# Banded attention and a gated dense layer on one core: the same instructions in another order

## The chip, the cores and the metric

The kernel runs on one core of a Trainium2 chip. The metric is the device time of one launch in microseconds (us). The kernel before takes 725.28 us, the median of three runs (724.6 to 726.31).

## The reference

The first half is attention over a band with a few sink columns: 4 batches, 8 heads, 768 positions, head size 64, `n_sink` 4 and `window` 128.

```
scores = np.matmul(q, k.transpose(0, 1, 3, 2)) / np.sqrt(D)
is_sink = pos[None, :] < n_sink
in_window = (rel >= 0) & (rel < window)          # rel = query position - key position
scores = np.where(is_sink | in_window, scores, -1e9)
a = softmax(scores); attn_out = a @ v             # (4, 8, 768, 64)
```

The second half takes the eight heads of a position as one row of 512 and puts it through two dense layers, with a gate between them:

```
x = attn_out.transpose(0, 2, 1, 3).reshape(3072, 512)
h = x @ w_in                                      # (3072, 2048)
g = h * np.cos(h)
out = g @ w_out                                   # (3072, 512)
```

`q`, `k` and `v` are float32. The weights arrive as 64-bit floats and are read as pairs of 32-bit words.

## The kernel before

**Tiles.** A float32 product is made of three TensorE products of parts: each operand is split into a high part and the low rest (`xhi`, `xlo`, `whi_in`, `wlo_in`, `ghi`, `glo`, `whi_out`, `wlo_out`), and high x high, high x low and low x high are summed in PSUM. The 3072 rows are cut into 12 chunks of 256 rows. The first four are the first 256 rows of each batch, whose heads are called early heads; they read keys and queries in their natural layout (L947) and turn them on TensorE (L955). The other eight chunks come later and share work between heads. Two chunks form a dense pair, d = 0 to 5, of 512 rows. A pair is worked off in 16 slots, one for each 128 columns of `h`. A slot is 12 matmuls of 128x512 into `h` (L476), a half sine on ScalarE (L485), a square (L491 on ScalarE or L493 on VectorE), the gate (L498), the split of g into `ghi` (L507, ScalarE) and `glo` (L514, VectorE), and 12 matmuls into four accumulators `acc` j = 0 to 3 (L523), which a later slot issues. In names such as `ghi_92` the number only tells allocations apart; `acc_80_1` is accumulator 1 of the last pair. The last slot keeps its g in the space of `whi_in`, so that its accumulator matmuls read `acc<-whi_out,whi_in`.

**Weights.** They come in 32 pieces of 128x512. A piece is loaded as pairs of words into one of two raw buffers (`raw0`, `raw1`, L580 on the SyncE queue), decoded on VectorE in three instructions (L595, L601, L607), rounded to its high part on ScalarE (L628), and its low part is taken by VectorE or GpSimd (L631). A load waits until its raw buffer is free, and what stands behind it on the SyncE queue waits with it.

**Checks.** The fast path holds only for inputs in some range. Late in the run the kernel reads weights again (L646) and values again (16 loads on SyncE, squares on ScalarE, L668, sums on VectorE, L671, all through the buffer `raw1` at the end) and gathers their extremes. When all are there, VectorE takes the maximum (L1665, L1669), TensorE turns it (`most_t`, L1675), VectorE reduces it (L1678), TensorE turns it again (`row_t`, L1682), and ten small VectorE instructions (L273 to L276, L1687 to L1697; the first four need nothing of the result) write the flag `redo`. Every engine then loads this flag into a register (`TENSOR_LOAD`, L1844) and branches on it (L1845): to a general path, which does not run with these inputs, or to the end of the program, which copies the last pair's four accumulators out of PSUM (L533 for j = 0 to 2 on ScalarE, for j = 3 one half by ScalarE, L543, and one by VectorE, L545) and stores them (L552).

**What sets the order.** No order is written by hand. Class `Plan` holds a list of steps, each with the engines that could do it, a planned duration, what it needs, and a priority (a planned time). `Plan.order` walks through planned time and lets each free engine take the ready step with the lowest key, which is the priority and penalties for a second choice of engine. The instructions of each engine then run on the chip in just that order. Priorities are made of the numbers in table `C`: `head_time(g)` from `TH`, `HB`, `TH2`, `HO` and `T`; `slot_time(d, s)` from `H0`, `STEP` and `T`; and offsets for the steps within a head or slot (`DQ`, `DS`, `DX`, `DH`, `DM`), the weight pieces (`WI`, `WO`, `WS`, `LEAD`) and the checks (`CK`, `CL`, `CV`, `CS`, `CT`, `CE`). Sixty idle matmuls (L1556) have the lowest priority and fill TensorE's first stretch. Three lines show the form:

```
i = add(dma(2), load_values, [r], prio - C["CL"], lat=2.6)
t, bt, bt2 = slot_time(len(ys) - 1, NFT - 1) + C["CE"], buf("tp", 1), buf("tp", 1)
i = add([("PE", 0.11)], most_turn, [i, bt], t)
```

Of the kernel before, what the change touches and what calls it, by code (L numbers as in the profile page):

```python
# [24 lines left out]
MASKED = 8.0e9  # L25

C = {
# [4 lines left out]
    "POOLF": 0.999, "POOLPEN": 2.492, "R": 2, "RAW": 2, "SAME": 0.056, "SEM": 0.352, "SPE": -0.019, "STEP": 7.601,  # L32
# [3 lines left out]
}  # L36
MAX_NORM = 39.0
MIN_TOP = 1.125 * 2.0**-15
# [1842 lines left out]
```

## Time and profile before

| | |
|---|---|
| Median of three runs | 725.28 us |
| Profiled execution | 727.14 us, span 725.3 us, granted clock 0.998 |
| Busy, share of the span | PE 707.8 us (98%), DVE 599.3 (83%), ACT 527.3 (73%), POOL 127.0 (18%) |
| Chain that ended last, by engine | PE 78%, ACT 12%, DVE 5%, issue 2%, DMA 2% |
| Traffic | HBM read 69.86 MB, written 6.29 MB |

The time of a run is the span of the profile and 1.84 us around it. The chain by engine says what the last work hung on: mostly TensorE (PE), and beside it ScalarE (ACT), VectorE (DVE) and a little DMA. A busy share is a mean over stages, so the rows below give the stages apart.

### The profile page before, as it was taken

The numbers are of one execution on the slowest core, as the hardware profiler recorded it, in microseconds if no ns is written. First come the engines' busy times: TensorE is split into PE (matmuls) and PEld (weight loads), VectorE is DVE, ScalarE is ACT, GpSimd is POOL, SyncE is SP. The second block draws the span as 40 slices with busy tenths as digits, with TensorE's granted clock in tenths as the row PEclk, the third lists the DMA queues.
The fourth block names the chain that finished last, engine by engine and source line by source line (L and its number), as shares of the span: only waits on it lengthen the run. The fifth ranks groups of instructions, "written<-read, shape, count | busy, mean of one in ns | idle before, by whom it ended". The sixth has DMA issues, their size and how long they took to land.

```text
span 725.3 us, 12983 instructions
## 1 busy us (share of the span) xinstructions
PE 707.8 (98%) x3674; PEld 583.6 (80%) x3674; DVE 599.3 (83%) x1850; ACT 527.3 (73%) x1344; POOL 127.0 (18%) x213
## 2 busy tenths in 40 slices
PE   7888999999999999999999999999999999999997
PEld 6766787888888888888888888888888888888885
DVE  6889999998988978988978989888988875567763
ACT  3796886787797697796686886877887856566652
POOL 1010000000333222232231232232122322100000
PEclk9999999999999999999999999999999999999999
DMA  5665565533255333355433254533244410375651
GB/s 144 177 181 162 140 178 148 155 67 66 63 118 130 86 67 54 64 125 128 93 58 59 42 144 101 122 63 62 44 124 107 111 35 12 96 198 158 167 138 63
DMA packets 236500, 77.11 MB, mean 106 GB/s; under 512 B 221060, under 2 KB 221060, under 8 KB 236420
## 3 DMA queue, kind: packets, MB, share of 16 engines
q1 hardware_dynamic: 236128, 75.15, 43.5%
q10 hardware_dynamic: 292, 1.05, 0.5%
q8 instruction: 31, 0.51, 0.3%
q14 instruction: 49, 0.40, 0.2%
HBM read 69.86 MB, written 6.29 MB: 105 GB/s over the span
## 4 chain that ended last, share of the span: by engine, by line
PE 78%; ACT 12%; DVE 5%; issue 2%; DMA 2%; SPq 0%; ACTq 0%; DVEq 0%
PE h L476 30%; PE acc L523 30%; PE av L1239 4%; PE s L1048 4%; ACT p L1079 3%; PE s L992 2%; PE tp L1160 2%; PE av L1215 2%; DMA xk<-in_k_dram 2%; ACT p L1097 1%; ACT L485 1%; ACT L1079 1%; PE qk L955 1%; PE tp L1170 1%; ACT early L390 1%
## 5 line engine op out<-in xcount | busy, mean ns | idle before, releaser
L523 PE MATMUL acc<-whi_out,ghi 128*128 128x512 f32 x376 | 158.7, 422 | 0.0
L476 PE MATMUL h<-xhi,whi_in 128*128 128x512 f32 x384 | 155.3, 405 | 0.0
L476 PE MATMUL h<-xlo,whi_in 128*128 128x512 f32 x384 | 150.9, 393 | 0.0
L476 PE MATMUL h<-xhi,wlo_in 128*128 128x512 f32 x384 | 150.1, 391 | 0.0
L523 PE MATMUL acc<-whi_out,glo 128*128 128x512 f32 x376 | 147.8, 393 | 0.0
L523 PE MATMUL acc<-wlo_out,ghi 128*128 128x512 f32 x376 | 147.1, 391 | 0.0
L1198 POOL TENSOR_SCALAR_AFFINE_SELECT ph<-ph 128x512 fp32r<-128x512 f32 x128 | 87.2, 681 | 230.9 <-DVE ph L1191 227.1
L485 ACT ACTIVATE r<-h 128x512 f32<-128x512 f32 x96 | 57.1, 598 | 47.9 <-PE h L476 45.3
L476 PEld LDWEIGHTS h<-xlo,whi_in 128*128 128x128 f32 x384 | 72.1, 188 | 16.2
L523 PEld LDWEIGHTS acc<-whi_out,glo 128*128 128x128 f32 x376 | 70.6, 188 | 15.8
L476 PEld LDWEIGHTS h<-xhi,whi_in 128*128 128x128 f32 x384 | 72.3, 188 | 12.0 <-DVE r L498 0.3
L476 PEld LDWEIGHTS h<-xhi,wlo_in 128*128 128x128 f32 x384 | 72.5, 189 | 11.3
L523 PEld LDWEIGHTS acc<-whi_out,ghi 128*128 128x128 f32 x376 | 71.4, 190 | 10.4
L1079 ACT ACTIVATE p<-p,st 128x136 f32<-128x136 f32 (+1 forms) x192 | 79.3, 415 | 0.3
L523 PEld LDWEIGHTS acc<-wlo_out,ghi 128*128 128x128 f32 x376 | 71.3, 190 | 9.2
L498 DVE SCALAR_TENSOR_TENSOR r<-r,h 128x512 f32<-128x512 f32 x96 | 64.5, 674 | 16.9 <-ACT r L491 16.3
L507 ACT CAST ghi<-r 128x512 fp32r<-128x512 f32 x94 | 58.2, 619 | 19.6 <-PE acc L523 12.7
L514 DVE TENSOR_TENSOR glo<-r,ghi 128x512 fp32r<-128x512 f32 x94 | 65.3, 694 | 5.6 <-ACT ghi L507 4.9
L1070 DVE CUSTOM_DVE_ANT_0 p<-s,mk 128x136 f32<-128x136 f32 (+1 forms) x192 | 59.7, 313 | 6.2 <-PE s L992 2.8
L1008 ACT CAST l<-tq 64x256 fp32r<-64x256 f32 x64 | 25.8, 403 | 46.9 <-PE s L1048 46.4
L1056 DVE COPY_PREDICATED s<-mk,s 128x128 f32<-128x128 int32 x128 | 37.2, 291 | 25.6 <-PE s L1048 23.7
L1048 PEld LDWEIGHTS s<-r,l 128*128 128x128 f32 x256 | 46.4, 188 | 12.3 <-DVE ph L1191 1.4
(161 smaller groups left out, 1314.7 us busy)
## 6 DMA issues: line engine op xcount, KB each, us to landing
xk<-in_k_dram SPq DMA_DIRECT2D x256, 48.0 KB
raw<-in_moe_w_out_dram SPq DMA_DIRECT2D x16, 512.0 KB
wt<-in_moe_w_in_dram SPq DMA_DIRECT2D x32, 256.0 KB
raw<-in_moe_w_in_dram SPq DMA_DIRECT2D x14, 512.0 KB
v<-in_v_dram SPq DMA_DIRECT2D x64, 96.0 KB
raw<-in_v_dram SPq DMA_DIRECT2D x32, 192.0 KB
out_dram<-wt SPq DMA_DIRECT2D x22, 256.0 KB
wt<-in_moe_w_out_dram SPq DMA_DIRECT2D x20, 256.0 KB
```

The costliest lines, as they stand in the source:

```text
L476: nc.tensor.matmul(out=o.h, lhsT=w[:, c, fs], rhs=xx[:, c, :], start=(c == 0 and n == 0), stop=(c == NC - 1 and n == 2),)
L485: nc.scalar.activation(out=o.r, in_=o.h, func=AF.Sin, scale=0.5)
L498: nc.vector.scalar_tensor_tensor(out=o.r, in0=o.r, scalar=0.5, in1=o.h, op0=ALU.subtract, op1=ALU.mult)
L507: nc.scalar.copy(out=o.ghi, in_=o.r)
L514: e.tensor_tensor(out=o.glo, in0=o.r, in1=f32(o.ghi), op=ALU.subtract)
L523: nc.tensor.matmul(out=y.acc[j], lhsT=gg[:, j * P : (j + 1) * P], rhs=w[:, f, :], start=(f == 0 and n == 0), stop=(f == NFT - 1 and n == 2),)
L1048: nc.tensor.matmul(out=o.s_ps[j][:, :w], lhsT=o.l[:, j * P : (j + 1) * P], rhs=r.rearrange("p n s -> p (n s)")[:, c0 : c0 + w], start=(n = ...
L1056: nc.vector.copy_predicated(out=o.s_ps[j][:, :P], mask=below.bitcast(I32), data=o.s_ps[j][:, SW : SW + P])
L1070: nc.vector.tensor_tensor_reduce(out=o.pj[j][:, :w], in0=o.s_ps[j][:, :w], in1=masks[min(o.i0 + j, 2)][:, :w], op0=ALU.add, op1=ALU.min, s ...
L1079: nc.scalar.activation(out=o.pj[j][:, :w], in_=o.pj[j][:, :w], func=AF.Exp, bias=o.lead.st[:, 0, o.nth, j : j + 1], scale=-1.0, accum_out= ...
L1198: nc.gpsimd.affine_select(out=ph[:, :, b, :], in_=f32(ph)[:, :, 1, :], pattern=[[0, 2 * CB], [(-1, 1)[b], P]], compare_op=(ALU.is_gt, ALU. ...
L1239: nc.tensor.matmul(out=dst, lhsT=lhs, rhs=rhs, start=(n == 0), stop=(n == len(seq) - 1), skip_group_check=True)
```

## The change

Only the table `C` differs. No step is added or taken away; the numbers that make the priorities are others, and the planner gives another order from them. Two lines of it:

```
-    "CT": 8.22, "CS": -0.257, "CE": -3.976, "H0": 21.541, "HB": 1.252, "TH2": 7.345, "GA": 16, "GHI": 2, "GLO": 2,
+    "CT": 14.939, "CS": -0.447, "CE": -7.191, "H0": 24.38, "HB": 0.716, "TH2": 7.156, "GA": 16, "GHI": 2, "GLO": 2,
...
```

Changed besides are `ALT`, `BLF`, `CK`, `DA`, `DH`, `DM`, `DQ`, `DS`, `DV`, `DX`, `CV`, `CL`, `HO`, `SX`, `CR`, `LEAD`, `NM`, `NW`, `NWF`, `PEN`, `POOLF`, `POOLPEN`, `SAME`, `STEP`, `T`, `TH`, `P0`, `A0`, `G0`, `S0`, `ZV`, `LD`, `HOT`, `RL`, `K2`, `WI`, `WO`, `WS`, `WS2` and `VP`. The table's `FILL`, `R`, `RAW`, `WT`, `PB`, `L` and the other buffer counts stay.

**TensorE, end of the list.** Before, the two turns of the check's result (`most_t`, `row_t`) stand between accumulator matmuls of slot 92's g, with 39 matmuls behind the second:

```order
L523 MATMUL acc_80_1_7949<-wlo_out_92,ghi_92_8472 128x512
L523 MATMUL acc_80_1_7949<-whi_out_91,glo_92_8485 128x512
L1675 MATMUL most_t_8534<-ident_77,most_93 33x128
L523 MATMUL acc_80_2_7956<-whi_out_91,ghi_92_8472 128x512
L523 MATMUL acc_80_2_7956<-wlo_out_92,ghi_92_8472 128x512
L523 MATMUL acc_80_2_7956<-whi_out_91,glo_92_8485 128x512
L1682 MATMUL row_t_8541<-ident_77,row_94 1x33
L523 MATMUL acc_80_3_7963<-whi_out_91,ghi_92_8472 128x512
```

After, the rows up to the branch are these:

```order
L523 MATMUL acc_80_3_7958<-whi_out_91,whi_in_89 128x512
L523 MATMUL acc_80_3_7958<-wlo_out_92,whi_in_89 128x512
L523 MATMUL acc_80_3_7958<-whi_out_91,whi_in_89 128x512 x2
L523 MATMUL acc_80_3_7958<-wlo_out_92,whi_in_89 128x512
L523 MATMUL acc_80_3_7958<-whi_out_91,whi_in_89 128x512
L1675 MATMUL most_t_8580<-ident_77,most_93 33x128
L1682 MATMUL row_t_8583<-ident_77,row_94 1x33
L1844 TENSOR_LOAD redo_86
L1845 COMPARE_AND_BRANCH
```

Both turns have moved behind the last accumulator matmul; nothing but the load of the flag and the branch follows them.

**VectorE, end of the list.** The last value sum (L671), the maxima and the work that leads to the flag; before, they stand ahead of the last slot's gate (`r_95`):

```order
L514 TENSOR_TENSOR whi_in_89<-r_94_8493,whi_in_89 128x512
L671 TENSOR_REDUCE yt_79<-raw1_71 128x12
L1665 TENSOR_REDUCE most_93<-yt_79 128x32
L1669 TENSOR_REDUCE most_93<-yt_79 128x1
L1678 TENSOR_REDUCE row_94<-most_t_8534 33x1
```

After, the gate and `glo` of the last slot (`whi_in`) come first, and the last value sum and the rest behind them:

```order
L671 TENSOR_REDUCE yt_79<-raw1_71 128x12
L498 SCALAR_TENSOR_TENSOR r_95_8523<-r_95_8523,h_95_8496 128x512
L514 TENSOR_TENSOR whi_in_89<-r_95_8523,whi_in_89 128x512
L671 TENSOR_REDUCE yt_79<-raw1_71 128x12
L1665 TENSOR_REDUCE most_93<-yt_79 128x32
L1669 TENSOR_REDUCE most_93<-yt_79 128x1
L1678 TENSOR_REDUCE row_94<-most_t_8580 33x1
L273 TENSOR_TENSOR lims_83<-sm_81,lims_83 1x4
```

The check's own chain is the same, but begins behind the last slot's work.

**SyncE, front of the list.** Loads of queries and keys for the early heads (`xq`, `xk`), raw weight pieces and values, from row 9 on. Before:

```order
L947 DMA xq_74<-in_q_dram 128x2x64 x2
L947 DMA xk_75<-in_k_dram 128x2x64 x2
L580 DMA raw1_71<-in_moe_w_in_dram 128x1024
L947 DMA xq_74<-in_q_dram 128x2x64 x2
L580 DMA raw0_70<-in_moe_w_out_dram 128x1024
L947 DMA xk_75<-in_k_dram 128x2x64 x2
L947 DMA xq_74<-in_q_dram 128x2x64 x2
L928 DMA vpe_153<-in_v_dram 128x2x64
L947 DMA xk_75<-in_k_dram 128x2x64 x2
L928 DMA v32_76<-in_v_dram 128x2x64
```

After:

```order
L947 DMA xq_74<-in_q_dram 128x2x64 x2
L947 DMA xk_75<-in_k_dram 128x2x64 x2
L580 DMA raw1_71<-in_moe_w_in_dram 128x1024
L947 DMA xq_74<-in_q_dram 128x2x64 x2
L947 DMA xk_75<-in_k_dram 128x2x64 x2
L580 DMA raw0_70<-in_moe_w_out_dram 128x1024
L928 DMA vpe_153<-in_v_dram 128x2x64
L947 DMA xq_74<-in_q_dram 128x2x64 x2
L947 DMA xk_75<-in_k_dram 128x2x64 x2
L928 DMA v32_76<-in_v_dram 128x2x64
```

The first load of a `w_out` piece (into `raw0`) now stands behind a pair of key loads instead of ahead of it, and the first value load (`vpe`) ahead of a pair of `xq` and a pair of `xk`.

**VectorE, front.** From the start to the copy `tk` (L392) that releases the score matmul ahead of the first dense matmul, VectorE's list had 129 instructions and now has 126: one each fewer of L595, L601 and L607, two fewer of L392 with 64x256, one fewer of L392 with 128x384, and three more of L1099 with 128x128. ScalarE's list up to the last high part of x (L349) that the first dense matmul reads had 92 instructions and now has 90. All 60 idle matmuls stand ahead of the first dense matmul in both orders, and one score matmul more does now. Slots 2 to 14 of the first pair have 2 to 4 us more of the heads' matmuls ahead of them than before; from slot 15 on the two orders are level again. Three low parts of `w_out` pieces (L631) go from VectorE to GpSimd.

## Rows read from the trace of the kernel before

**Rows 1.** Windows: stretch, its length, PE, PEld, DVE, ACT, POOL busy, clock, DMA share, GB/s

```profile
20.00:57.00 37.00, 32.30 (x187) 24.98 (x187) 31.04 (x108) 33.05 (x113) 3.43 (x4) 1.00 0.65 171
57.00:170.00 113.00, 110.79 (x554) 89.10 (x555) 105.34 (x283) 84.47 (x205) 1.22 (x4) 1.00 0.52 137
170.00:620.00 450.00, 448.75 (x2401) 373.32 (x2399) 383.87 (x1253) 346.54 (x903) 119.09 (x192) 1.00 0.39 83
620.00:720.50 100.50, 100.48 (x451) 81.86 (x449) 64.39 (x153) 56.95 (x106) 0.72 (x1) 1.00 0.52 141
```

**Rows 2.** Chain that ended last: start us, us, what

```profile
43.42 3.85 DMA xk<-in_k_dram
57.32 1.39 PE h L476 x6
...
711.37 9.12 PE acc L523 x39
...
720.51 0.39 ACT raw L543
...
721.01 0.42 DVE raw L545
```

**Rows 3.** Timeline of TensorE at the end: start us, us, instruction

```profile
710.29 0.27 PE L1675 MATMUL most_t<-ident,most 128*33 128x128 f32 x1
...
720.09 0.39 PE L523 MATMUL acc<-whi_out,whi_in 128*128 128x512 f32 x1
```

**Rows 4.** Timeline of VectorE at the end

```profile
702.04 0.95 DVE L671 TENSOR_REDUCE yt<-raw 128x12 f32<-128x768 f32 x1
...
708.11 0.95 DVE L671 TENSOR_REDUCE yt<-raw 128x12 f32<-128x768 f32 x1
...
709.37 0.21 DVE L1669 TENSOR_REDUCE most<-yt 128x1 f32<-128x64 f32 x1
...
712.29 0.15 DVE L1697 SCALAR_TENSOR_TENSOR redo<-row_t,sm 1x1 int32<-1x1 f32 x1
```

**Rows 5.** Line L533 from 700 us on: ScalarE's first instruction behind the branch

```profile
L533 ACTq EVENT_SEMAPHORE  x3: 17/17/937, 716.2 to 717.8; - x3
```

**Rows 6.** Flag's load, L1844: queue, ns min/median/max, first and last start us

```profile
L1844 POOLq TENSOR_LOAD <-redo x1: 489/489/489, 712.5 to 712.5; - x1
```

**Rows 7.** Branch, L1845, and GpSimd's first instruction behind it

```profile
L1845 POOLq COMPARE_BRANCH  x1: 45/45/45, 713.0 to 713.0; - x1
L1845 ACTq COMPARE_BRANCH  x1: 50/50/50, 713.6 to 713.6; - x1
...
L1845 POOLq EVENT_SEMAPHORE  x1: 17/17/17, 715.6 to 715.6; - x1
```

**Rows 8.** Timeline of ScalarE at the end

```profile
709.81 0.60 ACT L485 ACTIVATE r<-h 128x512 f32<-128x512 f32 x1 [1.73 <-PE h L476]
...
717.16 1.23 ACT L533 ACTIVATE wt<-acc 128x512 f32<-128x512 f32 x2 [3.48 <-PE acc L523]
```

**Rows 9.** VectorE by line and form up to 57 us: busy us, mean ns, idle before

```profile
L607 DVE SCALAR_TENSOR_TENSOR wt<-raw,wt 128x512 int32<-128x512 int32 x10 | 6.8, 683 | 0.1
...
L595 DVE TENSOR_SCALAR wt<-raw 128x512 int32<-128x512 int32 x10 | 4.2, 419 | 2.3 <-DMA raw<-in_moe_w_in_dram 2.2
L392 DVE COPY early<-qk 64x256 f32<-64x256 f32 x6 | 2.5, 425 | 3.3 <-ACT tk L390 1.7 <-PE qk L955 1.0 <-ACT early L390 0.6
...
L392 DVE COPY early<-tp 128x384 f32<-128x384 f32 x3 | 1.7, 553 | 0.0
...
L1099 DVE TENSOR_SCALAR p<-p,st 128x128 f32<-128x128 f32 x2 | 0.6, 282 | 0.0
```

**Rows 10.** Timeline of SyncE's queue in front: start us, us, DMA issue

```profile
19.86 1.71 SPq L580 DMA_DIRECT2D raw<-in_moe_w_out_dram  x1
21.67 0.90 SPq L947 DMA_DIRECT2D xk<-in_k_dram  x2
```

**Rows 11.** SyncE's waits up to 57 us: total us, times, longest us

```profile
SPq L928 <- PE av L1215: 3.3, 4, 1.2
```

More of the change, by code (lines that the diff above doesn't have):

```diff
@@ L27 @@
 C = {
[4 rows of a table removed]
-    "POOLF": 0.999, "POOLPEN": 2.492, "R": 2, "RAW": 2, "SAME": 0.056, "SEM": 0.352, "SPE": -0.019, "STEP": 7.601,
[3 rows of a table removed]
[4 rows of a table added]
+    "POOLF": 1.007, "POOLPEN": 3.979, "R": 2, "RAW": 2, "SAME": 0.061, "SEM": 0.352, "SPE": -0.019, "STEP": 7.814,
[3 rows of a table added]
 }
```

12 rows, old and new, of the table C are left out of this document.

## The prediction

> **What bounds the kernel now.** I read the windows by stage first. TensorE is the engine to watch: from 170 to 620 us it is idle for 1.25 us of 450, from 620 us to its last matmul for 0.02 of 100.5, and from 57 to 170 us for 2.2 of 113 [rows 1]. There a new order can give back nearly nothing, since the same matmuls take the same time. Idle time lies in two places: ahead of the first dense matmul at 57.3 us [rows 2], where TensorE does without 4.7 us of 37 and ScalarE (33.05 of 37) and VectorE (31.04 of 37) are as full [rows 1], and behind the last matmul. So I read the front and the end apart.
>
> At the end the chain of waits shows an unbroken run of 39 accumulator matmuls from 711.37 us on, then ScalarE's half copy at 720.51 and VectorE's, which ends at 721.43 [rows 2]. The last matmul starts at 720.09 [rows 3] and the span ends at 725.3, so 5.2 us lie behind it. The check's two turns stand far ahead of that: `most_t` at 710.29 [rows 3], the flag written at 712.29 + 0.15 = 712.44 [rows 4], and load, branch and jump were over on ScalarE at 716.2 [rows 5], while TensorE still had 4 us of matmuls in hand. All of the decision is hidden.
>
> **The change, the end.** In the new order both turns stand behind the last accumulator matmul. Neither the flag nor any branch can come before it, and the four copies and stores stand behind the branch. Counted from the start of the last accumulator matmul:
>
> - to `most_t`: one matmul spacing, 9.12/39 = 0.23 [rows 2];
> - `most_t` to the flag: 712.44 - 710.29 = 2.15 [rows 3, 4]. The four VectorE instructions that need nothing of the result still stand behind the first reduction, so this chain keeps its length;
> - flag to the end of the compare: load at 712.5 and 0.49 long [rows 6], compare 0.05 [rows 7], so 713.04 - 712.44 = 0.60;
> - the jump: ScalarE's compare ends at 713.65 [rows 7] and its first instruction behind it is at 716.2 [rows 5]: 2.55. It is no wait for data, since GpSimd, which has nothing to wait for, shows the same (713.0 + 0.05 to 715.6, [rows 7]);
> - three copies of 128x512 in a row on ScalarE at 1.23/2 [rows 8]: 1.85. Before, they were spread between the matmuls that fill the four accumulators;
> - ScalarE's half and VectorE's half: 721.43 - 720.51 = 0.92 [rows 2];
> - last store to the end of the span: 725.3 - 721.43 = 3.87.
>
> The sum is 12.17 us against 5.21 before, so 6.96 more. The two turns no longer stand between the accumulator matmuls; I take one matmul spacing, 0.23, for both, so that much comes off. **End: +6.7 us.** Bounds: 6.7 - 2.55 = 4.2, if the jump hides (rival C), and about 8, if the check's values come late (rival D).
>
> [...] The compares here take 45 to 50 ns, but the time to the next instruction decides.
>
> **The change, the front.** VectorE has three instructions fewer ahead of the copy that releases the first dense slot. One weight piece less is L595 0.42, L607 0.68 and L601, of the same form, 0.68: 1.79. Two copies of 64x256 at 0.425 are 0.85, one of 128x384 is 0.55, and three more normalisations at 0.28 come back, 0.85 [rows 9]: 1.79 + 0.85 + 0.55 - 0.85 = 2.34 us less. ScalarE has two instructions less, at its mean of 33.05/113 = 0.29 [rows 1] an estimated 0.6. On SyncE the load of a `w_out` piece held the queue for 1.71 us from 19.86, since its buffer was not free, and the key loads behind it went out at 21.67 only [rows 10]; now these keys go first, up to 1.7 us earlier, and a later key load stands in the chain with 3.85 us [rows 2]. Against that, the first value load, which waits for TensorE's `av` matmuls (3.3 us in four waits, the longest 1.2, [rows 11]), now stands ahead of queries and keys. The weight piece is not saved, only done later, between 57 and 170 us, where VectorE is busy for 105.3 of 113 [rows 1].
>
> So the bounds of the front: if ScalarE or the value load's wait decides, -0.6 or, with a late key pair, up to +2; if VectorE's saving counts in full and the chain's key load goes too, -2.3 - 3.85, about -6. **I take -2.3 us**, VectorE's sum, since its copies lie on the chain and the two changes on SyncE pull in opposite directions.
>
> **The middle.** Slots 2 to 14 of the first pair come 2 to 4 us of head matmuls later, which fills TensorE with other work in the same time and leaves VectorE more room for the later weight piece. TensorE's idle 2.2 us is all that could be won there [rows 1]; 3 us could be lost, if VectorE, with 7.7 us of room, falls behind with pieces. I take 0. From 170 us on, 0 with bounds of 1 either way: what TensorE was idle there is 1.25 us. The three low parts that go to GpSimd lie beside its idle time, 119 us of 450 busy even in its fullest stretch [rows 1]; without that cover they would return to VectorE's list.
>
> **Sum.** 6.7 - 2.3 + 0 = **+4.4 us**. Against the profiled execution this gives a span of 729.7 and a time of 731.5 (727.14 + 4.4); that execution stands 1.86 above the median of the runs, 725.28, so a median of **729.7 us**.
>
> **Rivals.**
>
> A is the forecast.
>
> B, the other side: the front swallows the end. TensorE's idle time ahead of the first dense matmul is what can be won; VectorE's list is shorter, and the keys come early. It decides if the first dense matmul comes more than 6.7 us before 57.3, by 50.6 us. With the bounds, -6 for the front and -2.2 for the middle, the net is 6.7 - 8.2 = -1.5, so 723.8 us; -6 alone gives 724 to 726. Against it: TensorE idles for only 4.7 us of those 37, ScalarE is busy for 33.05 of 37 and saves 0.6, and the idle matmuls all stand ahead of the first dense one as before. 0.13, of which 0.06 beyond the bound of "faster".
>
> C: the jump is hidden in the new place, too, or its target's code is there already. The end costs 4.2, the net is 1.9: 727.2 us. For it: the compare alone takes 0.05 us. Against it: both engines show 2.5 us with nothing else to wait for, and no instruction stands between load and jump. 0.13.
>
> D: the value check becomes the last thing that the end waits for. Its 15th sum now follows the last half sine, which runs from 709.81 for 0.60 [rows 8], and a square of 768 columns, by the 512-column copies' 0.615 [rows 8] an estimated 0.9, so it falls near 711.3 in the time of before; the 16th follows one load, square and sum later, 708.11 - 702.04 = 6.07 [rows 4], near 717.3, and the maxima are done 709.58 - 708.11 = 1.47 after that [rows 4], near 718.8. `most_t` can start at 720.3, so 1.5 us are left. If the load is late by more than that, or the first pair's pieces stall TensorE as said, 2 to 4 us come on top: about 732.7 us. 0.14.
>
> **How the numbers follow.** A has 0.60. What this kernel's measurement can tell from no change is 0.2%, 1.45 us, so "same" is 723.8 to 726.7. Faster holds B's 0.06; same the rest of B and the low edge of C and A, 0.10; slower 0.84. The range reaches from the middle of B and C to D: 726.3 to 733.0 us. A's own range, with the front between -4 and 0, is 728 to 732.
>
> **What would show it.** The last accumulator matmul, `most_t`, `row_t`, the flag, the load and the branch in a row, then a gap near 2.5 us on ScalarE, then three copies back to back; about 12.2 us from the last accumulator matmul's start to the end of the span, against 5.2. If VectorE's maxima end after the last accumulator matmul, D is right; if the gap is under 0.5 us, C. The first dense matmul near 55 us shows the front right; later than 57.3 shows it wrong, and earlier than 51 is B. TensorE's idle time from the first dense matmul to the last should stay near 3.5 us. If it grows to 6 or more, the middle was mis-sized.

## The result: 735.82 us, 10.3 us slower

The changed order takes 735.82 us (734.77 to 735.88, four runs) against 725.48 us before (now four runs); the ratio is 1.0139, with an interval of 1.0122 to 1.0157. A second set of runs gave 735.92 us, 1.0143 (1.0126 to 1.0160). The forecast was 729.7 us and the range ended at 733.0: the sign was right, the size was not.

The profiled execution took 735.88 us with a span of 734.2. First the windows of TensorE's stages (columns as in [rows 1]):

```profile
20.00:57.00 37.00, 32.88 (x197) 26.70 (x196) 32.63 (x118) 33.47 (x114) 2.20 (x3) 1.00 0.64 170
57.00:170.00 113.00, 110.19 (x550) 88.03 (x549) 105.51 (x282) 86.37 (x212) 6.21 (x8) 1.00 0.53 140
170.00:620.00 450.00, 448.52 (x2386) 373.46 (x2386) 382.78 (x1223) 349.11 (x916) 129.62 (x188) 1.00 0.38 82
620.00:728.00 108.00, 101.14 (x459) 82.79 (x457) 67.84 (x158) 55.26 (x104) 1.87 (x3) 0.99 0.48 128
728.00:734.20 6.20, 0.00 (x0) 0.00 (x0) 0.42 (x1) 0.93 (x3) 0.00 (x0) 0.50 0.49 169
```

Up to 620 us TensorE's busy times look like those of [rows 1]. What does not show as idle time shows in the counts: from 170 to 620 us TensorE issued 2386 matmuls where it had issued 2401. The large change is in the last two lines, where TensorE has nothing to do for over 12 us.

The end, on TensorE, then the flag on VectorE, in the timelines of the changed kernel:

```profile
720.46 0.39 PE L523 MATMUL acc<-whi_out,whi_in 128*128 128x512 f32 x1
720.69 0.27 PE L1675 MATMUL most_t<-ident,most 128*33 128x128 f32 x1
721.33 0.19 PE L1682 MATMUL row_t<-ident,row 33*1 33x33 f32 x1 [0.38 <-DVE row L1678]
```

```profile
718.77 0.21 DVE L1669 TENSOR_REDUCE most<-yt 128x1 f32<-128x64 f32 x1
...
722.58 0.15 DVE L1697 SCALAR_TENSOR_TENSOR redo<-row_t,sm 1x1 int32<-1x1 f32 x1
```

The last accumulator matmul starts at 720.46, 0.37 us later than before [rows 3]. The maxima are done at 718.98, 1.7 us ahead of the place where TensorE could turn them: rival D's wait did not come about. The flag is written at 722.73. Then the branch (L1845), and the first instruction behind it on ScalarE (L533):

```profile
L1845 ACTq COMPARE_BRANCH  x1: 50/50/50, 723.3 to 723.3; - x1
L1845 SPq COMPARE_BRANCH  x1: 45/45/45, 723.3 to 723.3; - x1
L1845 POOLq COMPARE_BRANCH  x1: 45/45/45, 723.3 to 723.3; - x1
L1845 PEldq COMPARE_BRANCH  x1: 3622/3622/3622, 723.4 to 723.4; - x1
L1845 DVEq COMPARE_BRANCH  x1: 72/72/72, 723.4 to 723.4; - x1
L1845 PEldq EVENT_SEMAPHORE  x1: 51/51/51, 727.0 to 727.0; - x1
L1845 POOLq EVENT_SEMAPHORE  x1: 17/17/17, 727.2 to 727.2; - x1
```

```profile
L533 ACTq EVENT_SEMAPHORE  x3: 17/17/17, 727.0 to 727.2; - x3
```

All five engines compare within 0.1 us, and none does anything until 727.0: a gap of 3.7 us, where GpSimd and ScalarE showed 2.55 us in [rows 5, 7]. There each engine jumped at a time of its own, with compares at 713.0, 713.3, 713.6, 714.4 and 716.9 us. At last the copies, and SyncE's stores:

```profile
727.08 1.09 ACT L533 ACTIVATE wt<-acc 128x512 f32<-128x512 f32 x2 [9.60 <-PEq L1845]
728.05 0.60 ACT L533 ACTIVATE raw<-acc 128x512 f32<-128x512 f32 x1
728.53 0.40 ACT L543 ACTIVATE raw<-acc 128x256 f32<-128x256 f32 x1
```

```profile
729.04 0.42 DVE L545 TENSOR_SCALAR raw<-acc 128x256 f32<-128x256 f32 x1 [6.32 <-ACT raw L543]
```

```profile
727.71 1.96 SPq L552 DMA_DIRECT2D out_dram<-wt  x2
729.85 0.85 SPq L552 DMA_DIRECT2D out_dram<-raw  x2
```

The last data are there at 729.46, but SyncE issues four stores in a row and gets to the last at 730.4. From the last accumulator matmul's start to the end of the span it is 734.2 - 720.46 = 13.7 us, before 5.2.

### The profile page after: what moved, and what is told of

Read it like the earlier page. It is cut to its first block, busy times and chain, and to the rows that moved or that the text cites. A ratio compares the mean times of both kernels' runs of the same rounds, so it can differ in the third digit from the quotient of the medians.

```text
span 734.2 us, 13059 instructions
## 1 busy us (share of the span) xinstructions
PE 708.7 (97%) x3674; PEld 585.6 (80%) x3674; DVE 601.8 (82%) x1829; ACT 532.0 (72%) x1364; POOL 142.0 (19%) x214
## 5 line engine op out<-in xcount | busy, mean ns | idle before, releaser
L523 PE MATMUL acc<-whi_out,ghi 128*128 128x512 f32 x376 | 157.1, 418 | 0.0
L476 PE MATMUL h<-xhi,whi_in 128*128 128x512 f32 x384 | 156.2, 407 | 0.0
L476 PE MATMUL h<-xlo,whi_in 128*128 128x512 f32 x384 | 150.6, 392 | 0.0
L476 PE MATMUL h<-xhi,wlo_in 128*128 128x512 f32 x384 | 149.9, 390 | 0.0
L1198 POOL TENSOR_SCALAR_AFFINE_SELECT ph<-ph 128x512 fp32r<-128x512 f32 x128 | 94.6, 739 | 223.2 <-DVE ph L1191 219.1
L476 PEld LDWEIGHTS h<-xlo,whi_in 128*128 128x128 f32 x384 | 72.1, 188 | 16.2
L476 PEld LDWEIGHTS h<-xhi,whi_in 128*128 128x128 f32 x384 | 72.2, 188 | 14.0 <-DVE r L498 1.4
L476 PEld LDWEIGHTS h<-xhi,wlo_in 128*128 128x128 f32 x384 | 72.4, 188 | 11.8
L1070 DVE CUSTOM_DVE_ANT_0 p<-s,mk 128x136 f32<-128x136 f32 (+1 forms) x192 | 60.0, 314 | 10.6 <-PE s L992 5.5
L1048 PEld LDWEIGHTS s<-r,l 128*128 128x128 f32 x256 | 46.3, 188 | 13.2 <-issue 1.9
L1048 PE MATMUL s<-r,l 128*128 128x264 f32 x256 | 54.3, 292 | 0.3
```

Source lines behind the costliest of these rows:

```text
L476: nc.tensor.matmul(out=o.h, lhsT=w[:, c, fs], rhs=xx[:, c, :], start=(c == 0 and n == 0), stop=(c == NC - 1 and n == 2),)
L523: nc.tensor.matmul(out=y.acc[j], lhsT=gg[:, j * P : (j + 1) * P], rhs=w[:, f, :], start=(f == 0 and n == 0), stop=(f == NFT - 1 and n == 2),)
L1048: nc.tensor.matmul(out=o.s_ps[j][:, :w], lhsT=o.l[:, j * P : (j + 1) * P], rhs=r.rearrange("p n s -> p (n s)")[:, c0 : c0 + w], start=(n = ...
L1070: nc.vector.tensor_tensor_reduce(out=o.pj[j][:, :w], in0=o.s_ps[j][:, :w], in1=masks[min(o.i0 + j, 2)][:, :w], op0=ALU.add, op1=ALU.min, s ...
L1198: nc.gpsimd.affine_select(out=ph[:, :, b, :], in_=f32(ph)[:, :, 1, :], pattern=[[0, 2 * CB], [(-1, 1)[b], P]], compare_op=(ALU.is_gt, ALU. ...
```

## The experiments

The times of one chip job are compared with runs of before on the same chip.

**Only the end of the new order, in the old one.** One dependency holds the turns back; nothing else moves but the last slot's two VectorE instructions.

```diff
-        i = add([("PE", 0.11)], most_turn, [i, bt], t)
+        i = add([("PE", 0.11)], most_turn, [i, bt, *env.lasts], t)   # lasts: the four last accumulator steps
```

> The order of before in all but the end: the two turns of the check's result are held behind the last accumulator matmul, as in the changed order. Theory (the end is the loss): from the last accumulator matmul's start to the end of the span 13.7 us instead of 5.2, so 725.5 + 8.5 = 734.0 us (733.2 to 734.8). Rival (the loss is the rest of the new order, and the end was hidden as I summed or less): with my sum of 6.7 it is 732.2; if the end is worth nothing, 725.5.

Measured: 732.84 us, ratio 1.0095 (1.0080 to 1.0110), so 7.0 us with an interval of 5.8 to 8.0. The theory's range (733.2 to 734.8) is missed; the number lies nearer to the 732.2 of my own sum. In its profile 13.5 us lie behind the last accumulator matmul's start, 8.2 more than before. But the turns also leave TensorE's list ahead of it: from the first dense matmul of slot 95 to the last accumulator matmul it takes 13.37 us instead of 13.88, here and in the changed kernel. So by the trace the end costs 8.2 - 0.5 = 7.7 us, within the measured interval. The end alone makes up most of the loss.

**The changed order without the decision**, in which the load of the flag, the branch and the general path are left out and the copies follow the accumulators.

```diff
-    again = nc.values_load(redo, min_val=0, max_val=1)
-    with tc.If(again > 0) as general:
-        with ExitStack() as ctx2:
-            general_path()
-    with general.Else():
-        emit(ends)
+    emit(ends)
```

> Leaves out the load of the flag, the branch and the general path; the check is still computed, with its turns last. Theory (the copies wait for the branch alone): copies follow their accumulators, 5.2 us behind the last matmul's start, so 727.3 us. Rival (the stores or the check's own work hold the end): 729 us or more, since the check's result is still written 2 us after the last accumulator matmul.

Measured: 725.92 us, 0.9998 (0.9989 to 1.0007): 9.9 us less than the changed kernel. The check's turns still stand last, and its work still ends behind the last matmul, but nothing waits for it:

```profile
719.73 0.60 ACT L533 ACTIVATE raw<-acc 128x512 f32<-128x512 f32 x1 [0.76 <-PE acc L523]
721.09 0.38 ACT L543 ACTIVATE raw<-acc 128x256 f32<-128x256 f32 x1 [0.76 <-PE acc L523]
```

ScalarE copies each accumulator as TensorE leaves it. So the price is that of waiting for the branch, not of the check. The time is 1.4 us below the theory's 727.3: in this profile 4.4 us lie behind the last accumulator matmul's start, not 5.2, and the turns' 0.5 us, which the theory left out, come off ahead of it.

**The old order without the decision**, by the same edit.

> The order of before without the load of the flag, the branch and the general path (left out); the check is still computed. Beside the changed order without them (725.92 us), this compares the two orders up to the last matmul with equal ends. Theory (besides its end, the changed order loses about 1.3 us between the first dense matmul and the last, which eats the 1.7 us it gains ahead): 724.6 to 725.0 us, 0.8 to 1.3 below 725.92. Rival (the two orders are equal up to the last matmul, and all of the loss is the end): 725.9.

Measured: 725.30 us, 0.9998 (0.9988 to 1.0007). Before, the decision cost nothing that can be measured. (Its profile has 4.25 us behind the last accumulator matmul's start instead of 5.24; the time does not show them.) Against 725.92 the two orders differ by 0.6 us, and by 0.3 when each is taken against its own runs of before (725.86 and 725.55). With 1.3 us lost ahead of slot 95, as the section on the prediction finds, the traces would make it 0.9 (1.3, less 0.5 for the turns, and 0.1 more at the end); each of the two ratios is known to some 0.7 us, so this neither shows the 1.3 us nor speaks against it.

**The checks earlier, in the changed order.** Two value checks are issued in slots 0 to 7 of the last pair instead of 0 to 3.

```diff
-                for _ in range(1 + (s < NFT // 4) if d == len(ys) - 1 else 0):
+                for _ in range(1 + (s < NFT // 2) if d == len(ys) - 1 else 0):
```

> The changed order in all but the last pair: slots 0 to 7 of it, instead of 0 to 3, issue two value checks, and the planner then sets the two turns 30 and 27 accumulator matmuls ahead of the last one (before: 42 and 39). Theory (the end is the loss): the end falls back to 5.2 us, 735.8 - 8.5 = 727.3 us. Rival (front and middle lose): 735 or more. If the front gain of 2.3 us that I forecast is there, 723.5 to 725.

Measured: 729.45 us (six runs, 727.27 to 730.47), 1.0044 (1.0029 to 1.0060): 6.4 us of the 10 come back, and the theory's 727.3 is missed. Of the rest, 1.7 us is a lead that is too short. The flag is written at 717.37, the last accumulator matmul starts at 721.82, and the five engines jump within 0.7 us of each other:

```profile
L1845 ACTq COMPARE_BRANCH  x1: 50/50/50, 717.9 to 717.9; - x1
...
L1845 POOLq EVENT_SEMAPHORE  x1: 17/17/17, 721.7 to 721.7; - x1
```

```profile
L533 ACTq EVENT_SEMAPHORE  x3: 17/17/38, 721.9 to 722.1; - x3
```

The jump is over at 721.9, when at least three accumulators have been ready, so that all copies come in a row behind it: 6.9 us from the last matmul's start to the end instead of 5.2.

**A longer lead.** Besides, the last two value checks are not loaded and squared (left out; their sums are set to zero), so that the turns stand 45 and 42 accumulator matmuls ahead of the last.

```diff
+        few = b * H + h >= B * H - 4
-        i = add(dma(2), load_values, [r], prio - C["CL"], lat=2.6)
-        j = add([("ACT", act(2 * NB * D))], norms, [i], prio)
+        i = add([("SP", 0.0)] if few else dma(2), (lambda e: None) if few else load_values, [r], ...)
+        j = i if few else add([("ACT", act(2 * NB * D))], norms, [i], prio)
```

> The changed order with value checks in slots 0 to 7 and without the loads and squares of the last two value checks (left out; their sums are set to zero), which sets the two turns 45 and 42 accumulator matmuls ahead of the last. Theory (the decision is free once the flag is written some 9 us ahead of the last matmul; 27 matmuls, 6.2 us, were too few): end about 5.2 us, 725.9 us, as without the decision. Rival (front or middle of the changed order lose): 727 or more.

Measured: 726.93 us, 1.0018 (1.0008 to 1.0028): 1.0 us above the theory's 725.9, at the edge of the rival's 727. The decision is hidden: the flag is written at 711.76, the last accumulator matmul starts at 720.09, and 4.8 us lie behind that. What is left against before, 1.3 us (0.6 to 2.0), lies ahead of the end, and the rival is right about where. The run also does two loads and squares less, so it is no pure measure of that loss.

**Which part of the table loses ahead of the end?** Three kernels take a part of the numbers from one table and the rest from the other: start and pace from the new one, weight pieces from the new one, and, in the changed order with early checks, the step offsets of the old one.

```diff
-    ... "H0": 21.541, "HB": 1.252, "TH2": 7.345, ... "T": 6.724, "TH": 7.177, ...     # before_new_pace
+    ... "H0": 24.38, "HB": 0.716, "TH2": 7.156, ... "T": 6.759, "TH": 6.915, ...
-    ... "LD": -1.348, "RL": 7.549, "WI": -10.57, "WO": 8.749, "WS": 1.523, ...        # before_new_weights
+    ... "LD": 3.161, "RL": 7.942, "WI": -10.504, "WO": 9.188, "WS": 0.525, ...
-    ... "DQ": 3.932, "DS": -5.331, "DM": -0.933, "DV": -1.037, "NM": 0.337, ...       # after_old_offsets
+    ... "DQ": 3.964, "DS": -6.226, "DM": -1.278, "DV": 0.57, "NM": 3.042, ...
```

> Before with the changed table's numbers for start and pace alone (H0, TH, HB, TH2, HO, STEP, T, CR, the engines' starting times and HOT); step offsets, choice of engine, weights as before; the two turns stay 42 and 39 accumulator matmuls ahead of the end. Theory (the pace brings the earlier front, the offsets and choices the stalls behind it): first dense matmul near 55 us, stalls from 57 to 100 us as before, 724.2 us. Rival (the pace brings the stalls too): 726.5 to 727.

> Before with the changed table's numbers for the weight pieces alone (WI, WO, WS, WS2, LEAD, LD, RL). Up to row 304 of TensorE's list nothing moves. Theory (the weight pieces are not what costs): 725.9 within 0.7 us. Rival (pieces that come later stall the first pair): 727 or more.

> The changed order with the check values early (turns 30 and 27 ahead, 729.45 us) and with the step offsets of before (DQ, DS, DX, DA, DV, DH, DM, SX, K2, ZV, VP, NM). Theory (the extra 1.7 us of stalls on TensorE from 57 to 100 us come from the offsets): these stalls go, 727.7 us. Rival (they come from pace or choice of engine): stalls stay, 729.4 us.

Measured: 743.95 us (1.0255), 743.25 us (1.0236) and 743.20 us (1.0257). All times that the theories and rivals gave were missed: each mixture is 18 us slower than before, and after_old_offsets 14 us slower than after_checks_early, from which it was made. One part of a theory held: in before_new_pace the first dense matmul comes at 53.7 us, so the numbers for start and pace bring the earlier front. The time goes in stretches that neither whole table has. Here are windows of after_old_offsets, then of before_new_pace:

```profile
400.00:440.00 40.00, 34.03 (x160) 27.23 (x159) 32.39 (x100) 23.92 (x66) 12.79 (x20) 0.87 0.41 95
```

```profile
400.00:440.00 40.00, 36.70 (x189) 29.16 (x188) 34.14 (x108) 28.06 (x70) 12.54 (x21) 1.00 0.45 108
...
520.00:560.00 40.00, 36.29 (x181) 29.71 (x180) 33.49 (x109) 29.70 (x75) 9.92 (x15) 0.91 0.43 102
```

TensorE idles for 3 to 6 us of 40, where it idled for 1.25 us of 450 in [rows 1], and in two of the stretches the mean granted clock is 0.87 and 0.91. The numbers of a table are fitted to each other; one part of it says nothing about itself. What they do show: in after_old_offsets TensorE's waits from 57 to 100 us are those of the changed kernel, shown below, so the step offsets do not cause them.

**Is the jump dearer because five engines jump at once?** First, TensorE is kept busy with 40 small transposes behind the flag, and branches 2.5 us later than the others (GpSimd, which was to be held too, branched with the others).

```diff
+        def pe_rest(e):
+            for _ in range(40):
+                nc.tensor.transpose(out=tp, in_=most, identity=ident)
```

> TensorE gets 40 small transposes and GpSimd three memsets of its own behind the check, so that these two branch some 4 us after the others. Theory 1 (five engines that jump at once slow each other, 3.7 us instead of 2.55): ScalarE's gap falls toward 2.6 to 3.2 us and the time to 734.7 to 735.3. Theory 2 (ScalarE's first copy waits for TensorE's jump): the gap grows by 4 us, 739.5 us. Theory 3 (the jump is dearer at this place for every engine by itself): gap 3.7, 735.8 us.

Measured: 735.78 us (733.92 to 737.13). ScalarE's gap was 2.9 us instead of 3.7 (compare at 722.16, first instruction at 725.09), as theory 1 had it, but the time did not fall: from the issue of the last store (728.25) to the end of the span it took 5.5 us, where the changed kernel took 3.8. Why is not shown; TensorE's branch, the last here, ended at 728.4. GpSimd's gap was 3.3 us:

```profile
L1854 POOLq COMPARE_BRANCH  x1: 45/45/45, 722.1 to 722.1; - x1
...
L1854 POOLq EVENT_SEMAPHORE  x1: 17/17/17, 725.5 to 725.5; - x1
```

Then 20 small activations were to hold back ScalarE alone:

> The changed order; ScalarE gets 20 activations of one element behind the check, so that it branches alone, some 4 us after the other engines. Theory (a jump alone takes 2.55 us, five at once 3.7): ScalarE's gap from its compare to its first copy is 2.5 to 2.6 us, time 735.8 + 4 - 1.1 = 738.7 us. Rival (3.7 us is the price at this place): gap 3.7, time 739.8 us.

Measured: 734.73 us; inconclusive. Five of the activations stood ahead of the branch and 15 behind the copies, and ScalarE branched with the others (gap 4.1 us). So ScalarE was made to wait for VectorE by a semaphore:

```diff
+        def dve_rest(e):
+            for _ in range(8):
+                nc.vector.tensor_single_scalar(out=mk[:, :512], in_=mk[:, :512], scalar=0.5, op=ALU.mult)
+        def act_rest(e):
+            nc.scalar.activation(out=row[0:1, 0:1], in_=mk[0:1, 0:1], func=AF.Square)
```

> The changed order; behind the flag VectorE does eight multiplications of 128x512 on the masks, which nothing reads any more, and ScalarE waits for the last of them with one activation of one element, so that ScalarE loads the flag and branches alone, some 4 to 5 us after the other engines. Theory (a jump alone takes 2.55 us, five at once 3.7): ScalarE's gap from its compare to the first instruction behind it is 2.5 to 2.6 us. Rival (3.7 us is the price of the jump at this place): 3.6 to 3.9 us.

Measured in one run: 738.14 us, beside 726.58 us for before. GpSimd, TensorE and SyncE branched first, VectorE and ScalarE 3 us later:

```profile
L1852 POOLq COMPARE_BRANCH  x1: 45/45/45, 723.4 to 723.4; - x1
L1852 PEldq COMPARE_BRANCH  x1: 3442/3442/3442, 723.4 to 723.4; - x1
L1852 SPq COMPARE_BRANCH  x1: 45/45/45, 723.7 to 723.7; - x1
L1852 POOLq EVENT_SEMAPHORE  x1: 17/17/17, 726.1 to 726.1; - x1
...
L1852 ACTq COMPARE_BRANCH  x1: 50/50/50, 727.0 to 727.0; - x1
```

GpSimd's gap was 2.65 us, ScalarE's 3.4 us (727.08 to its copy at 730.44). For ScalarE neither theory holds. GpSimd's gaps fall in line over thirteen profiles: 2.5 to 2.7 us where at most SyncE jumps within 0.3 us of it ([rows 7], after_long_lead), 2.65 us here with TensorE and SyncE beside it, 3.3 us beside three others (after_jumps_apart), 3.6 us in after_old_offsets, where TensorE jumps 0.6 us behind the rest, and 3.7 to 4.0 us where all five jump together. That points to the company, though not to whether the number of the others counts or which they are. For ScalarE, whose gaps were between 2.5 and 4.1 us, it stays open what sets them.

**The last stores on two queues.** The second and third go out on ScalarE's queue.

```diff
-            nc.sync.dma_start(out=out[r0 : r0 + P, :], in_=y.o[j])
+            (nc.scalar if y.d == len(chunks) // 2 - 1 and j in (1, 2) else nc.sync).dma_start(out=..., in_=y.o[j])
```

> The changed order; the second and third of the last four stores are issued on ScalarE's queue instead of SyncE's. Theory (SyncE issues the four in a row, and the last one leaves 0.9 us after its data is there): the last store leaves at once, but ScalarE's two issues of some 0.35 us push its own copies; 0 to 0.5 us less, 735.3 to 735.8. Rival (the end is the transfer itself): 736.2 or more, since the copies come later.

Measured: 735.32 us, within the theory's 735.3 to 735.8. The last store leaves 0.04 us behind its data, but ScalarE's half copy starts 2.65 us behind its first copy instead of 1.45, since it issues two stores of 0.35 us each between its copies. The queue's 0.9 us are real, and this way gains nothing with them.

**The changed kernel again.**

> The changed kernel once more, unchanged, beside the others. Theory (the end costs 8.5 to 9 us, of which before_turns_late showed 7.0 within 5.8 to 8.0): 734.5 to 736. Rival (the first runs were high by chance): 733 to 734.

Measured: 735.92 us, 13.5 us behind the last accumulator matmul's start.

## Why the prediction was wrong in size

**The end, +6.7: right in kind, too small.** Step by step in the profile of the changed kernel, forecast in brackets: to `most_t` 0.23 (0.23), to the flag 2.04 (2.15), to the end of the compare 0.62 (0.60), the jump, up to the first copy, 3.73 (2.55), the three copies 1.45 (1.85), the two halves 0.93 (0.92), to the end of the span 4.74 (3.87). The sum is 13.7 against 12.2. For the turns that leave the matmuls, 0.5 us came off (0.23), so the end cost 13.7 - 5.2 - 0.5 = 8.0 us, 1.3 more than forecast. Two terms were mis-sized, the jump and the last store. The jump was taken from engines that jumped one after the other, and TensorE's own row before had a branch of 3942 ns that I did not use. That it costs the same in the new place was my estimate, and the runs showed 3.73 us there. The compares took 45 to 72 ns on four engines, and the next instruction came 3.7 us later. In that gap the trace of the changed kernel has five DMA packets on queues that it lists as instruction, four on q14 and one on q8, which start between 724.2 and 724.6 us. That the jump waits for them is not shown, and neither is rival C's other ground, that the target's code is there already. The last store was taken to leave behind its data, as it does where the four copies are spread, while SyncE took 1.96 us for the first two issues in a row and 0.85 us for the next two.

**The front, -2.3: right, in part by luck.** The first dense matmul (first start on L476) came at 57.1, 55.9 and 56.3 us in three profiles with the old front, 56.4 on the mean, and at 53.5 to 55.3 us, 54.4 on the mean, in nine with the new one: 2.0 us earlier. (before_new_weights, whose order is the old one up to there, has 55.5; with it, 1.8.) In the changed kernel's profile VectorE's copy `tk` starts at 53.25 us instead of 56.30, 3.05 earlier, where the sum had 2.34. Four `av` and two score matmuls now stand behind the score matmul that it releases, ahead of the first dense one, and take 1.1 us of it back; they were not in the sum. No run takes VectorE's saving apart from the rest. The three show also that the front of one order varies by over a microsecond between executions, and the one on which the forecast rested was the latest. I took 1.86 us off for that by going over to the median, and the changed kernel's profiled execution stands at its median: 735.88 to 735.82.

**The middle, 0: wrong.** This is the step that failed. From the first dense matmul to the first one of slot 95 it takes 649.1, 648.6 and 649.2 us in the old order and 651.9 to 652.9 us, 652.3 on the mean of nine, in the new: 3.3 us more, which eats the front's 2.0 and leaves 1.3. after_long_lead measured 1.3 us too, with the reservation made there. The two ends of this stretch, first in before, then in the changed kernel:

```profile
57.08 0.48 PE L476 MATMUL h<-xhi,whi_in 128*128 128x512 f32 x1
...
706.21 0.39 PE L476 MATMUL h<-xhi,whi_in 128*128 128x512 f32 x1
```

```profile
55.13 0.58 PE L476 MATMUL h<-xhi,whi_in 128*128 128x512 f32 x1
...
707.09 0.39 PE L476 MATMUL h<-xhi,whi_in 128*128 128x512 f32 x1
```

My bounds were taken from TensorE's visible idle time, with 3 us for VectorE falling behind on the first pair and 1 us from 170 us on. The idle time of the old order bounds what a new order can win; it says nothing of what it can lose. The sign that I had named did not show the loss either: from the first dense matmul to the last accumulator matmul TensorE was idle for 4.3 us (665.33 less 661.04 busy), not 6. The starts of equal slots, counted from the first dense matmul, show it. On the mean the new order is 1.4 us behind at slot 24 (where the heads' work is level again), 2.0 at slot 48, 2.5 at slot 64 and 3.3 from slot 84 on. Part of the loss lies in the first pair, where new waits stand; here those of before_no_decision and of the changed kernel from 57 to 100 us (total us, times, longest):

```profile
PE av L1215 <- ACT early L390: 0.7, 2, 0.4
PE s L992 <- ACT tk L390: 0.5, 1, 0.5
PE s L992 <- DVE st L1070: 0.4, 1, 0.4
```

```profile
PE qk L955 <- DVE st L1070: 1.0, 2, 0.5
PE av L354 <- ACT xhi L349: 0.8, 1, 0.8
PE s L992 <- DVE st L1070: 0.6, 2, 0.5
```

The turns of queries and keys now wait for VectorE's L1070; what makes that late is not shown. The windows of the same stretch, in the same order:

```profile
57.00:100.00 43.00, 41.39 (x208) 32.93 (x207) 40.58 (x104) 32.36 (x74) 0.31 (x1) 1.00 0.56 165
```

```profile
57.00:100.00 43.00, 40.40 (x203) 32.06 (x202) 39.54 (x107) 33.48 (x84) 1.59 (x2) 1.00 0.55 160
```

TensorE is busy for 40.40 us of the 43 instead of 41.39, and does 203 matmuls instead of 208. The other part lies late, where little shows as idle. The windows from 345 to 625 us, of before_no_decision and of the changed kernel:

```profile
345.00:625.00 280.00, 279.36 (x1497) 232.41 (x1497) 236.21 (x768) 211.54 (x548) 73.22 (x116) 1.00 0.36 78
```

```profile
345.00:625.00 280.00, 278.90 (x1487) 232.26 (x1486) 233.85 (x740) 217.15 (x573) 83.06 (x118) 1.00 0.36 78
```

TensorE is nearly as busy, and does ten matmuls fewer. Matmul ends are modelled and overlap the next start (the last accumulator matmul is shown as 0.39 us long, and `most_t` starts 0.23 us after it), so that a part of a short wait hides inside the busy time. TensorE's waits from 180 us on, in before and in the changed kernel, name the place:

```profile
PE tp L1160 <- DVE st L1070: 0.9, 4, 0.2
```

```profile
PE av L1239 <- ACT tk L390: 0.5, 3, 0.2
PE av L1239 <- POOL ph L1198: 0.4, 1, 0.4
```

The first `av` matmul of a later head (L1239) follows a score matmul (L1048) 51 times between slots 16 and 84. In the old order it starts 0.12 or 0.13 us behind it every time. In the new one six of them, at 326, 367, 439, 480, 552 and 592 us, start 0.34 to 0.67 us behind, 2.0 us more in all, and about half of that shows as idle. By the profile three wait for GpSimd's `ph`, which itself had waited for VectorE (L1191), and three for ScalarE's L390. The longest:

```profile
591.66 0.40 PE L1048 MATMUL s<-r,l 128*128 128x264 f32 x2
592.45 0.39 PE L1239 MATMUL av<-ph,vr 128*128 128x256 f32 x1 [0.38 <-POOL ph L1198]
```

These six waits are as much as the new order loses between slots 24 and 84. No run takes them away alone, so this is read from the traces.

**The sum.** -2.0 + 3.3 + 8.0 is 9.3 of the 10.3 us measured. The three profiled executions of the old order lie 0.7 us above the medians of their kernels on the mean, those of the new order at theirs, which is most of the rest. Of the rivals, B and C are wrong (no gain swallowed the end, and the jump is not hidden), D's wait for the value sums did not come, but its other half, stalls in the first pair, did, with 1 to 2 us instead of 2 to 4. The end alone is 7.7 us by the trace in the old order and 8.0 in the new one, against 7.0 (5.8 to 8.0) measured; leaving out the decision gave back 9.9, since the end without it is 4.4 us long. What the runs do not settle is what sets ScalarE's jump, and what makes VectorE late in the first pair.

## What to carry to other kernels

A decision that every engine must take before the last outputs leave has a lead time: here, as an estimate, the flag had to be written some 6 us ahead of the last matmul's start (in after_checks_early a lead of 4.45 us cost 1.7, which is 6.2 in all). With 7.65 us of lead it cost nothing that can be measured, with 8.3 the end was 4.8 us long, and behind the last matmul the flag cost 8. When an order is changed, look first at where such a step stands against the last work of the engine that bounds the kernel, and price the whole chain behind it, with the queue that must now do in a row what was spread before. In a list order that a planner makes from a table of fitted numbers, compare when equal slots start, not the idle time, and do not take the idle time that there is for the most that can be lost. Do not judge a part of the table by itself: each mixture of two good tables was 18 us slower than before.

## What the hardware showed

On ScalarE and GpSimd the time from the end of a compare to the first instruction behind the branch was 2.5 to 4.1 us, and TensorE's branch took 3.4 to 3.9 us in all thirteen profiles with a branch, while the compare itself took 45 to 72 ns on the other four engines. GpSimd's gap was longer where more engines jumped beside it, from 2.5 to 4.0 us. In after_old_offsets, from 400 to 440 us, TensorE idled for 6 us of 40 at a mean granted clock of 0.87.
